# Banded attention and a gated convolution layer: a rewritten schedule, the convolution in array quarters, q and k over 96 partitions

## The chip, the cores and the metric

The kernel runs on one core of a Trainium2 chip. The core has a TensorE (matmuls, written PE in the profile; its weight loads are PEld), a VectorE (DVE), a ScalarE (ACT), a GpSimd (POOL) and a SyncE (SP), which here only issues DMAs. Each engine executes its own instructions in program order and waits on semaphores for the others. A matmul multiplies a stationary operand of up to 128 rows and 128 columns with a moving operand and writes to PSUM, which has 8 banks of 512 float32 per partition. The metric is the device time of one execution in microseconds, lower is better, as the median of several runs.

## The reference

Attention over 8 batches, 8 heads, 576 positions, head size 64, then a gated layer over the 512 channels that the heads make together. Heads 0 to 3 look at the last 32 positions; heads 4 to 7 look at every fourth position of the last 128, which is again 32 positions.

```python
rel = pos[:, None] - pos[None, :]
mask_plain = (rel >= 0) & (rel < 32)
mask_dil = (rel >= 0) & (rel < 128) & (rel % 4 == 0)
scores = np.where(mask, q @ k.T / 8, -1e9)          # mask by head
x = (softmax(scores) @ v)                           # heads side by side: [8, 576, 512]
for kk in range(5):                                 # causal, one weight per channel and tap
    gate_pre += conv_w[kk] * xp[:, kk:kk + 576, :]
gate = 1 / (1 + np.exp(-gate_pre))
out = (gate * (x @ w_val)) @ w_out
```

Inputs and output are float32. The kernel computes in bfloat16 with float32 accumulation.

## The kernel before

The unit of attention is a pair: one batch and two neighbouring heads, so that two times 64 channels fill 128 partitions. There are 32 pairs, four in each batch, two plain and two dilated (`is_dil`). Because a dilated head sees only positions of its own remainder modulo 4, its 576 positions fall into four sequences of 144, in each of which it is a plain band of 32.

`load_qk` and `load_v` bring the next pair but one from SyncE. q and k come as 144 rows of four positions (1,024 bytes each), the first 96 rows on 96 partitions and the other 48 in a second tile, for the dilated pairs with a DMA for each head. Plain v comes in rows of one position (256 bytes). `convert` casts on GpSimd: q and k of the plain pairs, v of the dilated ones. The others are used without a cast: `hi_bf16` views the upper half of each float32 as bfloat16.

`transpose_in` turns q and k so that channels lie on partitions: eight TensorE transposes for each of q and k of a plain pair (four of 96 rows, four of 48), six of 96 rows for a dilated one, then a copy from PSUM (L179 on ScalarE for plain k, L182 on VectorE else). `scores` multiplies k and q, one matmul for each head on its own 64 rows of the array, takes the exponential (L212) and multiplies with the mask (L219); each pair has two halves, `hf`. `attn_v` multiplies with v, which has a column of ones for the sum, and divides (L251, L256). `transpose_x` turns the result back to channels on partitions: six transposes of 96 rows for a plain pair (L275), and for a dilated one four of 96 rows and four of 48 in turns (L269, L271), then a copy to `xT` (L278).

The gated layer works on groups of up to 512 positions. `conv_unit` computes 128 channels of the convolution: for each of five taps a matmul with a diagonal 128 by 128 matrix (L303), then the gate as a tanh (L307). `val_unit` is the product with `w_val` (L315) and the multiplication with the gate (L320). `out_unit` multiplies 128 positions with `w_out` (L329), evicts with ScalarE (L332) and stores from ScalarE's queue (L333).

Order is given by hand: each step of the loop issues the loads of pair i + 2, the scores of pair i, some items of the gated layer (`fill`, by a budget of 3.2 for each step and a cost for each kind), the product with v, the transposes of pair i + 1, again some items, and `transpose_x`. What is left of the gated layer follows after the loop. PSUM has two tiles of two banks for scores and products with v, and four single banks for all else.

Of the kernel before, what the change touches and what calls it, by code (L numbers as in the profile page):

```python
# [11 lines left out]


def _ceil_div(a, b):
    return (a + b - 1) // b


def hi_bf16(ap: bass.AP) -> bass.AP:
    b = ap.bitcast(BF16)
    idx = tuple([slice(None)] * (len(b.shape) - 1) + [slice(1, None, 2)])  # L20
    return b[idx]


@with_exitstack
def kernel(
# [16 lines left out]
    R = 4  # L42
    W = 32
    TT = S // R
    P0, P1 = 96, TT - 96
    scale = 1.0 / float(D) ** 0.5
    NCH = Dm // 128
    NG = H // 2
    NT = S // 96
    SB = S + 4  # L50
    CB = B * SB
    NTOK = B * S
    HALF = 288

    consts = ctx.enter_context(tc.tile_pool(name="consts", bufs=1))
    inbuf = ctx.enter_context(tc.tile_pool(name="inbuf", bufs=4))
    work = ctx.enter_context(tc.tile_pool(name="work", bufs=3))
    moe_sb = ctx.enter_context(tc.tile_pool(name="moe_sb", bufs=6))
    outbuf = ctx.enter_context(tc.tile_pool(name="outbuf", bufs=4))
    ps_s = ctx.enter_context(tc.tile_pool(name="ps_s", bufs=2, space=bass.MemoryType.PSUM))  # L60
    ps_m = ctx.enter_context(tc.tile_pool(name="ps_m", bufs=4, space=bass.MemoryType.PSUM))

    def bank(dt=FP32):
        return ps_m.tile([128, 512 if dt == FP32 else 1024], dt, name="bank")


    NKT_, NVP, NVD, NET = 3, 3, 2, 4
    kTs = [consts.tile([128, 640], BF16, name=f"kT{i}") for i in range(NKT_)]
    ets = [consts.tile([128, 2, 384], BF16, name=f"et{i}") for i in range(NET)]
    vps = [consts.tile([128, NT, 2, D + 1], FP32, name=f"vp{i}") for i in range(NVP)]  # L70
    vd0 = [consts.tile([96, 2, R, D + 1], BF16, name=f"vda{i}") for i in range(NVD)]
    vd1 = [consts.tile([80, 2, R, D + 1], BF16, name=f"vdb{i}") for i in range(NVD)]
    xT = consts.tile([128, NCH, CB], BF16, name="xT")
    y_all = consts.tile([128, NCH, NTOK], BF16, name="y_all")

    ident_b = consts.tile([128, 128], BF16, name="ident_b")
    ident_f = consts.tile([8, 8], FP32, name="ident_f")
    mask_d = consts.tile([128, HALF], BF16, name="mask_d")
    mask_p = consts.tile([128, 2, HALF], BF16, name="mask_p")


    order = [(b, g) for b in range(B) for g in ((2, 3, 0, 1) if b == 0 else (0, 2, 1, 3))]
    nat = {}
    cnt = {"p": 0, "d": 0}
# [4 lines left out]
    def load_qk(i):  # L89
        b, g = order[i]  # L90
        t = {}
        for name, src in (("q", q), ("k", k)):
            rows = src[b, 2 * g:2 * g + 2].rearrange("h (p r) d -> p h (r d)", r=R)
            a = inbuf.tile([P0, 2, R * D], FP32, name=f"{name}a")
            nc.sync.dma_start(out=a, in_=rows[0:P0])
            if is_dil(i):
                z = inbuf.tile([2 * P1, R * D], FP32, name=f"{name}zd")
                for hh in range(2):
                    nc.sync.dma_start(out=z[hh * P1:(hh + 1) * P1], in_=rows[P0:TT, hh, :])
            else:  # L100
                z = inbuf.tile([P1, 2, R * D], FP32, name=f"{name}zp")
                nc.sync.dma_start(out=z, in_=rows[P0:TT])
            t[name] = (a, z)
        nat[i] = t

    def load_v(i):
        b, g = order[i]
        t = nat[i]
        if g >= NG // 2:
            rows = v[b, 2 * g:2 * g + 2].rearrange("h (p r) d -> p h (r d)", r=R)  # L110
            a = inbuf.tile([96, 2, R * D], FP32, name="va")
            nc.sync.dma_start(out=a, in_=rows[0:96])
            z = inbuf.tile([80, 2, R * D], FP32, name="vz")
            nc.sync.dma_start(out=z, in_=rows[64:144])
            j = cnt["d"] % NVD
            cnt["d"] += 1
            t["v"] = (a, z, vd0[j], vd1[j])
        else:
            vt = vps[cnt["p"] % NVP]
            cnt["p"] += 1  # L120
            vv = v[b, 2 * g:2 * g + 2]
            nc.sync.dma_start(out=vt[:, 0, :, 0:D],
                              in_=vv[:, 0:128, :].rearrange("h p d -> p h d"))
            for hh in range(2):
                nc.sync.dma_start(
                    out=vt[:, 1:NT, hh, 0:D],
                    in_=bass.AP(tensor=v.tensor,
                                offset=v.offset + ((b * H + 2 * g + hh) * S + 64) * D,
                                ap=[[D, 128], [96 * D, NT - 1], [1, D]]))
            t["v"] = (vt,)  # L130

    def convert(i):
        if is_dil(i):
            a, z, c0, c1 = nat[i]["v"]
            for src, dst in ((a, c0), (z, c1)):
                nc.gpsimd.tensor_copy(  # L136
                    dst[:, :, :, 0:D], src.rearrange("p h (r d) -> p h r d", r=R))
        else:
            for name in ("q", "k"):
                res = []  # L140
                for src, n, x in zip(nat[i][name], (P0, P1), "az"):
                    c = work.tile([n, R, 2, D], BF16, name=f"{name}c{x}")
                    nc.gpsimd.tensor_copy(
                        c.rearrange("p r h d -> p h r d"),
                        src.rearrange("p h (r d) -> p h r d", r=R))
                    res.append(c)
                nat[i][name] = tuple(res)

    def transpose_in(i, name):
        a, z = nat[i][name]
        ps = bank(BF16)
        if is_dil(i):
            av, zv = hi_bf16(a), hi_bf16(z)
            pv = ps[:, 0:S].rearrange("p (f h t) -> p f h t", f=2, h=2)
            for f in range(2):
                cols = slice(f * 128, f * 128 + 128)
                for hh in range(2):  # L160
                    nc.tensor.transpose(out=pv[:, f, hh, 0:P0], in_=av[:, hh, cols],
                                        identity=ident_b[0:P0, 0:P0])
                nc.tensor.transpose(out=pv[:, f, :, P0:TT], in_=zv[:, cols],  # L163
                                    identity=ident_b[0:2 * P1, 0:2 * P1])
        else:
            for r in range(R):
                nc.tensor.transpose(out=ps[:, r * TT:r * TT + P0],
                                    in_=a[:, r, :, :].rearrange("p h d -> p (h d)"),
                                    identity=ident_b[0:P0, 0:P0])
            for r in range(R):  # L170
                nc.tensor.transpose(out=ps[:, r * TT + P0:(r + 1) * TT],  # L171
                                    in_=z[:, r, :, :].rearrange("p h d -> p (h d)"),
                                    identity=ident_b[0:P1, 0:P1])
        if name == "k":
            dst = kTs[i % NKT_]
        else:
            dst = work.tile([128, S], BF16, name="qT")
        if name == "k" and not is_dil(i):
            nc.scalar.copy(out=dst[:, 0:S].rearrange("p (t r) -> p t r", r=R),  # L179
                           in_=ps[:, 0:S].rearrange("p (r t) -> p t r", r=R))  # L180
        else:
            nc.vector.tensor_copy(dst[:, 0:S], ps[:, 0:S])  # L182
        nat[i][name + "T"] = dst

    state = {}

    def scores(i, hf):
        b, g = order[i]
        dil = g >= NG // 2
        qT, kT = nat[i]["qT"], nat[i]["kT"]  # L190
        ps = ps_s.tile([128, 2, 512], FP32, name="sc")
        qr = qT.rearrange("p (r t) -> p r t", r=R)

        def mm(out_c, ln, lhs, rhs):
            for x in range(2):
                rb = slice(x * D, x * D + D)
                nc.tensor.matmul(out=ps[:, x, out_c:out_c + ln], lhsT=lhs[rb], rhs=rhs[rb],  # L197
                                 start=True, stop=True)
        if dil:
            for hh in range(2):  # L200
                o = (2 * hf + hh) * TT
                mm(hh * 96, 96, kT[:, o:o + 128], qT[:, o:o + 96])
            for hh in range(2):
                o = (2 * hf + hh) * TT
                mm(192 + hh * 48, 48, kT[:, o + 64:o + 192], qT[:, o + 96:o + TT])
        else:
            for c in range(3):
                t = 3 * hf + c
                k0 = 0 if t == 0 else 96 * t - 32
                mm(c * 96, 96, kT[:, k0:k0 + 128], qr[:, :, 24 * t:24 * t + 24])  # L210
# [261 lines left out]
    while queue:  # L472
        run_item()
# [30 lines left out]
```

## Time and profile before

| what | value |
|---|---|
| three runs | 228.67, 231.15, 233.42 us (median 231.15) |
| profiled execution, span from first to last instruction | 223.8 us |
| ScalarE exponentials, L212 | 64 of 660 ns |
| VectorE masks, L219 | 64, median 458 ns |
| VectorE division, L256 | 32 of 686 ns, 32 of 553 ns |
| copies from PSUM: L278, L179 (ScalarE), L182 (VectorE) | 637, 638, 444 ns |
| tanh L307, eviction L332 (ScalarE), product with the gate L320 (VectorE), each 128x512 | 599, 601, 679 ns |
| GpSimd casts of 96x512, L136 and L143 | 622 to 662 ns |
| SyncE issues of loads | 240 |
| ScalarE issues of stores | 36 |

The profile is of one execution; its time as the host measures it is not recorded beside its span. The median of the runs lies 7.35 us above the span. "Busy" is time in which an engine had at least one instruction under way. A TensorE matmul's own duration contains the time that its results take to arrive, so the rate of a stream is read from one start to the next and not from the duration of one. The clock row tells what share of its full clock TensorE was granted.

### The profile page before, as it was taken

Reading aid. Unit: us, or ns where it says so; the run is one execution under the profiler, and the core shown is the slowest. Engines: PE = TensorE matmul, PEld = TensorE weight load, DVE = VectorE, ACT = ScalarE, POOL = GpSimd, SP = SyncE. Lnnn points to the kernel's source line nnn. Section 1 sums busy time; section 2 is a strip of 40 time slices with the busy share of each in tenths; the row PEclk is TensorE's granted clock in tenths of the full one; section 3 lists DMA queues with packets and bytes.
Section 4 is the critical chain, followed back from the end, with each engine's and each line's share of the span. In section 5 each row is a group of like instructions: output and inputs, shape, how many; then the busy total and the mean of one; then the engine's idle time right before and its main releaser. Section 6 shows DMA issues by size and latency. Waiting matters only on the chain.

```text
span 223.8 us, 5850 instructions
## 1 busy us (share of the span) xinstructions
PE 189.1 (85%) x2279; PEld 127.0 (57%) x2292; DVE 128.4 (57%) x311; ACT 108.7 (49%) x190; POOL 65.0 (29%) x123
## 2 busy tenths in 40 slices
PE   2666689878988898898898898889888988999992
PEld 0544545545655576556775686558655666454670
DVE  2566664775667556663666659656776566532320
ACT  2234444356554655475544753465536654643442
POOL 4296506420516150524146024602360200000000
PEclk9999999999999999996999999999999999999999
DMA  5799999747779799869989779778986300221232
GB/s 144 240 220 207 236 216 225 211 120 232 213 212 231 234 254 224 217 222 258 233 192 243 234 217 237 181 244 227 232 213 212 118 3 0 99 91 47 100 141 94
DMA packets 58757, 41.82 MB, mean 187 GB/s; under 512 B 29029, under 2 KB 54117, under 8 KB 58730
## 3 DMA queue, kind: packets, MB, share of 16 engines
q1 hardware_dynamic: 52480, 30.95, 56.1%
q10 hardware_dynamic: 5194, 9.45, 11.8%
q0 software_dynamic: 1056, 1.05, 2.9%
q8 instruction: 18, 0.29, 0.6%
q14 instruction: 9, 0.07, 0.1%
HBM read 33.04 MB, written 9.44 MB: 190 GB/s over the span
## 4 chain that ended last, share of the span: by engine, by line
PE 45%; DMA 15%; ACT 13%; DVE 10%; issue 7%; SPq 6%; ACTq 2%; POOL 0%; DVEq 0%
PE bank L303 16%; ACT et L212 9%; PE bank L315 8%; PE bank L329 5%; DVE et L219 4%; ACT osb L332 4%; DMA qa<-in_q_dram 4%; DVE xn L256 4%; DMA vp<-in_v_dram 3%; PE bank L269 3%; PE sc L246 2%; PE bank L271 2%; DMA ka<-in_k_dram 2%; ACTq L333 2%; DMA kzd<-in_k_dram 2%
## 5 line engine op out<-in xcount | busy, mean ns | idle before, releaser
L303 PE MATMUL bank<-xT,conv_diag 128*128 128x320 bf16 (+7 forms) x319 | 46.3, 295 | 0.3 <-DMA kzd<-in_k_dram 0.3
L256 DVE TENSOR_TENSOR xn<-sc,rec 96x512 bf16<-96x512 f32 (+1 forms) x64 | 39.7, 620 | 2.2
L212 ACT ACTIVATE et<-sc 128x576 bf16<-128x576 f32 x64 | 38.5, 660 | 4.8 <-PE sc L197 4.8
L307 ACT ACTIVATE gate<-bank 128x512 bf16<-128x512 f32 (+3 forms) x40 | 22.0, 556 | 32.8 <-PE bank L303 32.8
L315 PE MATMUL bank<-xT,w_val_b 128*128 128x320 bf16 (+7 forms) x254 | 37.1, 285 | 0.3 <-issue 0.3
L136 POOL CAST vda<-va 96x512 bf16<-96x512 f32 x16 | 10.0, 622 | 92.9 <-DMA va<-in_v_dram 79.3
L332 ACT ACTIVATE osb<-bank 128x512 f32<-128x512 f32 x36 | 21.6, 601 | 29.4 <-PE bank L329 23.4
L320 DVE SCALAR_TENSOR_TENSOR y_all<-gate,bank 128x512 bf16<-128x512 bf16 (+3 forms) x40 | 25.1, 628 | 18.0 <-PE bank L315 9.1
L303 PEld LDWEIGHTS <-conv_diag 128*128 128x128 bf16 x320 | 27.8, 100 | 12.6 <-issue 1.4
L329 PE MATMUL bank<-w_out_b,y_all 128*128 128x512 bf16 x134 | 33.7, 380 | 0.8 <-DVE y_all L320 0.2
L219 DVE TENSOR_TENSOR et<-et,mask_d 128x576 bf16<-128x576 bf16 x32 | 16.7, 524 | 27.9 <-ACT et L212 26.9
L278 ACT COPY xT<-bank 128x576 bf16<-128x576 bf16 x32 | 20.4, 637 | 23.1 <-PE bank L271 17.8
L219 DVE TENSOR_TENSOR et<-et,mask_p 128x576 bf16<-128x576 bf16 x32 | 16.8, 532 | 25.6 <-ACT et L212 24.6
L315 PEld LDWEIGHTS <-w_val_b 128*128 128x128 bf16 x256 | 20.8, 97 | 8.1
L329 PEld LDWEIGHTS <-y_all 128*128 128x128 bf16 x144 | 12.8, 98 | 14.4 <-DVE y_all L320 1.8
L179 ACT COPY kT<-bank 128x576 bf16<-128x576 bf16 x16 | 10.2, 638 | 20.4 <-PE bank L171 16.4
L236 PE MATMUL sc<-vda,et 96*128 96x65 bf16 x128 | 12.2, 203 | 7.6 <-DVE et L219 3.7
L246 PE MATMUL sc<-vp,et 128*128 128x65 bf16 x192 | 12.1, 201 | 7.5 <-DVE et L219 4.2
L269 PE MATMUL bank<-ident_b,xn 96*128 96x96 bf16 x64 | 14.1, 221 | 4.4 <-DVE xn L256 4.4
L251 DVE RECIPROCAL rec<-sc 96x8 f32<-96x8 f32 (+1 forms) x64 | 12.2, 191 | 9.5 <-PE sc L246 7.7
L182 DVE COPY qT<-bank 128x576 bf16<-128x576 bf16 x32 | 14.2, 444 | 3.3 <-PE bank L163 3.0
L236 PEld LDWEIGHTS <-et 96*128 96x128 bf16 x128 | 8.1, 100 | 14.1 <-DVE et L219 13.6
(62 smaller groups left out, 243.5 us busy)
## 6 DMA issues: line engine op xcount, KB each, us to landing
out_dram<-osb ACTq DMA_DIRECT2D x36, 256.0 KB, 2.3
qa<-in_q_dram SPq DMA_DIRECT2D x32, 192.0 KB, 4.1
ka<-in_k_dram SPq DMA_DIRECT2D x32, 192.0 KB, 3.4
vp<-in_v_dram SPq DMA_DIRECT2D x32, 160.0 KB, 3.8
va<-in_v_dram SPq DMA_DIRECT2D x16, 192.0 KB, 3.6
vz<-in_v_dram SPq DMA_DIRECT2D x16, 160.0 KB, 3.8
qzd<-in_q_dram SPq DMA_DIRECT2D x32, 48.0 KB, 3.4
kzd<-in_k_dram SPq DMA_DIRECT2D x32, 48.0 KB, 3.1
```

What stands on the lines that cost most here:

```text
L212: nc.scalar.activation(out=et[:, :, 0:HALF], in_=ps[:, :, 0:HALF], func=AF.Exp, scale=scale)
L219: nc.vector.tensor_tensor(out=ev, in0=ev, in1=for_mask, op=ALU.mult)
L236: nc.tensor.matmul(out=ps[:, x, hh * DA:(hh + 1) * DA], lhsT=et[0:96, x, hh * 96:hh * 96 + 128], rhs=c0[:, hh, r, :], start=True, stop=True)
L256: nc.vector.tensor_tensor(out=xo, in0=av[:, :, :, 0:D], in1=rec[:, :, 0:n, None].to_broadcast([96, 2, n, D]), op=ALU.mult)
L269: nc.tensor.transpose(out=pv[:, r, 0:96], in_=xn[:, 2 * r, :, :].rearrange("p h d -> p (h d)"), identity=ident_b[0:96, 0:96])
L278: nc.scalar.copy(out=xT[:, g, c0:c0 + S].rearrange("p (t r) -> p t r", r=R), in_=pv.rearrange("p r t -> p t r"))
L303: nc.tensor.matmul(out=ps[:, o:o + ln], lhsT=conv_diag[:, c, kk, :], rhs=xT[:, c, s:s + ln], start=(kk == 0), stop=(kk == K - 1))
L307: nc.scalar.activation(out=gate[:, 0:n], in_=ps[:, 0:n], func=AF.Tanh, scale=0.5)
L315: nc.tensor.matmul(out=ps[:, o:o + ln], lhsT=w_val_b[:, mc, c * 128:(c + 1) * 128], rhs=xT[:, mc, col:col + ln], start=(mc == 0), stop=(mc ...
L320: nc.vector.scalar_tensor_tensor(out=y_all[:, c, t0:t0 + n], in0=gate[:, 0:n], scalar=1.0, in1=ps[:, 0:n], op0=ALU.add, op1=ALU.mult)
L329: nc.tensor.matmul(out=ps[0:n, :], lhsT=y_all[:, c, t0:t0 + n], rhs=w_out_b[:, c, :], start=(c == 0), stop=(c == NCH - 1))
L332: nc.scalar.activation(out=osb[0:n, :], in_=ps[0:n, :], func=AF.Copy, scale=0.5)
```

## The change

The kernel is written anew. The costs that stand in its code are figures of its planner and are not used as times here. The list of its parts:

- **Order.** Each piece of work is a `Task` with a cost, dependencies, a priority and a number of PSUM banks. `Plan.run` places the tasks one after the other on a model of the engines and picks the engine where a task may run on two; the program is emitted in that order. It models SyncE's queue too, with at most eight transfers in flight.
- **PSUM.** One tile of eight banks; a task takes one bank or any two and gives them back after its eviction.
- **Loads.** q and k lie on 96 partitions: dilated in rows of 12 positions (3,072 bytes), plain in rows of six (1,536 bytes), one DMA each; six buffers for each of q and k, where there were four. Plain v's first block has 96 rows where it had 128.
- **Attention.** Six transposes of 96 rows for each of q and k, of both kinds. k is reordered when it is copied from PSUM, in the dilated pairs also. One mask multiplication of 1,152 columns for a pair, in place of two of 576; VectorE or GpSimd. The division of a plain pair is one operation over six blocks. `transpose_x` of a dilated pair has eight transposes of 96 rows.
- **Gated layer.** It goes by whole batches in halves of 288 positions. The convolution uses 64 by 64 diagonal matrices: rows 0 to 63 and 64 to 127 of the array, for each the columns of one of the two halves, so that four matmuls address four quarters. In the second half of positions the two halves of the 128 channels are exchanged, and `w_val` and `w_out` are kept in a second, exchanged copy for it. The output takes four tiles of 128 positions for each batch, and after four batches two more made of the 32 positions that each half leaves.
- **Stores.** From SyncE's queue, between the loads; 36 as before, and two DMAs that make the exchanged `w_out`. SyncE issues 144 loads, 36 stores and these two. ScalarE or VectorE evicts the output and q, k and x.

```diff
+class Plan:
+    def run(self):
...
+                    e = min(t.cost, key=lambda e: max(ready, free[e]) + t.cost[e])
+                    est = max(ready, free[e])
+                    if e == "SP":
+                        live = sorted(x for x in flight if x > est)
+                        if len(live) >= self.FLIGHT:
+                            est = live[-self.FLIGHT]
...
+    PS = psum.tile([128, 8, 512], FP32, name="ps")
...
+    NQ, NV, NET, NX, NO = 6, 4, 3, 3, 6
...
+    order = [(b, g) for b in range(B) for g in ((2, 0, 3, 1) if b == 0 else (0, 2, 1, 3))]
...
+            if dil:
+                s = two.rearrange("h (p r) d -> (h p) (r d)", r=12)
+                d = dst
+            else:
+                s = two.rearrange("h (p r) d -> p h (r d)", r=6)
+                d = dst.rearrange("p (h c) -> p h c", h=2)
+            P["l" + nm] = ld("ld" + nm, i + (0.0 if nm == "q" else 0.1), 295.0, 300.0,
+                             lambda t, d=d, s=s: nc.sync.dma_start(out=d, in_=s), [dep])
...
+    def transpose_in(t, i, src):
+        ps = bank(t, BF16)
+        if is_dil(i):
+            for f in range(6):
+                nc.tensor.transpose(out=ps[:, f * 96:f * 96 + 96],
+                                    in_=hi_bf16(src)[:, f * 128:f * 128 + 128],
+                                    identity=ident[0:96, 0:96])
+        else:
+            for j in range(6):
+                nc.tensor.transpose(out=ps[:, j * 96:j * 96 + 96],
+                                    in_=src[:, j, :, :].rearrange("p h d -> p (h d)"),
+                                    identity=ident[0:96, 0:96])
...
+    def exps(t, ps, et, hf):
+        nc.scalar.activation(out=et[:, hf * 576:hf * 576 + 576].rearrange("p (b c) -> p b c", b=2),
+                             in_=ps[:, :, 0:HALF], func=AF.Exp, scale=scale)
+    def masks(t, i, et):
+        eng = nc.vector if t.engine == "DVE" else nc.gpsimd
+        eng.tensor_tensor(out=et[:, 0:ET], in0=et[:, 0:ET], in1=(mask_d if is_dil(i) else mask_p)[:, 0:ET],
+                          op=ALU.mult)
...
+    def transpose_x(t, i, xn, xm):
+        ps = bank(t, BF16)
+        if is_dil(i):
+            for part in (1, 0):
+                sv = (xn, xm)[part].rearrange("p n h d -> p (n h d)")
+                for rho in range(2):
+                    for hf in range(2):
+                        o = (rho * 2 + hf) * 128
...
+                        nc.tensor.transpose(out=dst, in_=sv[:, o:o + 128], identity=ident[0:96, 0:96])
...
+        mk = P["mk"] = add("mk", i, {"DVE": 1.05, "POOL": 2.4}, lambda t: masks(t, i, et),
+                           exs + [K_sd if dil else K_sp])
...
+    def conv(t, b, c):
+        ps = banks(t, 2)
+        for kk in range(K):
+            for half in range(2):
+                for x in range(2):
+                    ob = (x ^ half) * D
+                    s = b * SB + half * HALF + kk
+                    nc.tensor.matmul(out=ps[ob:ob + D, half, 0:HALF],
+                                     lhsT=conv_d[x * D:x * D + D, c, kk, :],
+                                     rhs=xT[x * D:x * D + D, c, s:s + HALF],
+                                     start=(kk == 0), stop=(kk == K - 1))
+    def val(t, b, c):
+        ps = banks(t, 2)
+        for half in range(2):
+            s = b * SB + 4 + half * HALF
+            for mc in range(NCH):
+                nc.tensor.matmul(out=ps[:, half, 0:HALF], lhsT=w_val[half][:, mc, c * 128:(c + 1) * 128],
+                                 rhs=xT[:, mc, s:s + HALF], start=(mc == 0), stop=(mc == NCH - 1))
...
+    def out_tile(prio, half, cols, deps, store):
...
+        ot = add("ot", prio, {"PE": 0.87}, lambda t: outp(t, half, cols), list(deps) + K_wo[half], banks=1, mode="full")
+        oe = add("oe", prio, {"ACT": 0.60, "DVE": 0.69}, lambda t: evict_o(t, bank(ot), osb),
+                 [ot] + (out_st[n - NO] if n >= NO else []), frees=[ot])
+        sts = [add("st", prio, {"SP": 0.45}, lambda t, e=e: e(osb), [oe], lag=(nb, 340.0)) for e, nb in store]
...
+    def gated(b):
+        base = 4 * b + 3
...
+            cv = add("conv", base + 1.0 + 0.5 * c, {"PE": 0.62}, lambda t, c=c: conv(t, b, c), [ev[c], K_cd], banks=2, mode="half")
...
+            vl = add("val", base + 1.2 + 0.5 * c, {"PE": 0.98}, lambda t, c=c: val(t, b, c), list(ev.values()) + K_wv, banks=2, mode="full")
...
+    for b in range(B):
+        for i in range(4 * b, 4 * b + 4):
+            attend(i)
+        gated(b)
+    for t in plan.run():
+        t.emit(t)
```

## The prediction, made before the changed kernel ran

> **What bounds the kernel now.** I read the slices of the span first, then busy times by stage, the chain of waits, and single stretches of TensorE.
>
> ```profile
> PE   2666689878988898898898898889888988999992
> PEclk9999999999999999996999999999999999999999
> DMA  5799999747779799869989779778986300221232
> ```
>
> Three phases: a start in which the DMA row is full and PE is not, a long middle with PE at 8 to 9, and an end with PE full and DMAs nearly idle. The stages, cut where each batch's convolution starts (columns: stretch, length, then busy us of each engine, clock, DMA share, GB/s):
>
> ```profile
> 0.00:32.00 32.00, 18.65 (x229) 13.28 (x231) 18.61 (x62) 10.69 (x18) 16.20 (x43) 1.00 0.98 209
> 55.80:79.30 23.50, 21.00 (x290) 13.25 (x284) 14.85 (x34) 12.72 (x23) 8.30 (x13) 1.00 0.79 224
> 102.20:127.30 25.10, 22.90 (x296) 16.42 (x293) 14.98 (x34) 13.12 (x23) 8.83 (x15) 0.94 0.95 243
> 195.40:223.80 28.40, 23.82 (x146) 13.85 (x146) 7.35 (x15) 11.19 (x22) 0.00 (x0) 1.00 0.25 93
> ```
>
> The span is 32.0 + 7 periods of 23.34 + 28.4. In a period PE is busy 21.0 of 23.5 us, VectorE 14.9, ScalarE 12.7: PE bounds the middle, with DMAs at 0.79 behind it. The first batch waits for loads; the end is gated-layer work left over. The chain in a period and at its end (start, us, what):
>
> ```profile
> 55.94 2.30 PE bank L303 x20
> ...
> 59.15 0.87 PE bank L315 x8
> 60.02 1.10 PE bank L303 x10
> ...
> 63.81 0.17 PE bank L167 x4
> 63.98 0.20 PE bank L171 x4
> 64.18 0.28 PE bank L167 x4
> 64.46 0.20 PE bank L171 x4
> ```
>
> The convolution costs 1.10 us for 512 positions and 128 channels, val 0.87. PE alone, start, duration, line:
>
> ```profile
> 60.96 0.42 PE L275 MATMUL bank<-ident_b,xn 96*128 96x96 bf16 x6
> 61.31 0.44 PE L197 MATMUL sc<-qT,kT 64*128 64x96 bf16 x16
> 61.69 0.29 PE L315 MATMUL bank<-xT,w_val_b 128*128 128x64 bf16 x4
> ...
> 197.14 0.21 PE L269 MATMUL bank<-ident_b,xn 96*128 96x96 bf16 x1
> 197.28 0.19 PE L271 MATMUL bank<-ident_b,xn 48*128 48x48 bf16 x1
> 197.41 0.22 PE L269 MATMUL bank<-ident_b,xn 96*128 96x96 bf16 x1
> ```
>
> Six transposes of 96 rows last 0.42 us; one lasts 0.21, so they start 0.042 us apart. The sixth starts at 61.17 and the first score at 61.31, 0.14 later: going over to 64 rows costs about 0.10. L269 and L271 pay this at every step, since 48 rows take the 64-row form: they start 0.13 to 0.14 apart.
>
> **The change part by part**, against the span, in us of each period (one batch: two plain pairs, two dilated, 576 positions of the gated layer).
>
> *Convolution.* Now 4 x 1.10 x 576/512 = 4.95. In quarters, if all four run side by side, half the columns: 2.48. The row that it is nearest to is L197: 16 matmuls on two row halves, 0.44 in all, less a last one of about 0.18, is 0.26, or 0.033 for each pair of 96 and 48 columns in turn, with both weight loads: two halves do run together. Four quarters no row shows. The bounds: two at a time, 4.95, no gain; four, a gain of 2.47. For weight loads the nearest row is L315 with 64 columns: four loads and matmuls with starts 0.03 apart, (0.29 - 0.19)/3; four loads of a tap would take 0.12 beside 288 columns that take 0.215 x 288/512 = 0.12 (val's 0.87/4 for 512), just hidden. I take four. Eight changes of form at 0.10 are added at most (0.8), none if each convolution stands beside scores; I take 0.5. Gain 1.97; lower bound a loss of 0.8.
>
> The page "TensorEngine Tiling (Array Packing)", section Restrictions and Gotchas, says that column tiling excludes fast weight loads, and "TensorE: Matmul & The Clock Gate", section LDWEIGHTS, gives columns / 1.2 ns without them: by estimate 53 ns for 64 columns, 213 for the four of a tap if one follows the other, which would make the convolution 4.3 and the gain 0.2. The first page also says that different row tiles cannot access one PSUM bank at the same time; here the two row tiles of a half do write one bank, on different partitions. No run here shows either in quarters.
>
> *Transposes.* Of dilated x: eight that take 1.09 (197.14 to the next item at 198.23) become eight of 96 rows, 0.34: 0.75 twice, 1.5. Of plain q and k: 0.17 + 0.20 + 0.28 + 0.20 = 0.85 become 12 x 0.042 = 0.50: 0.35 twice, 0.7. Dilated ones stay at 12.
>
> *Val, output, scores, products with v* keep their columns: nothing on PE. Output has 36 tiles as before.
>
> PE: 21.0 - 1.97 - 1.5 - 0.7 = 16.8 a period. With the 2.5 that it is now idle, 19.3; with convolution at its bounds 18.3 to 22.1.
>
> *VectorE.* Masks 8 x 0.53 become four of 1,152 columns, about 2 x 0.458 each: -0.5; dilated k goes from L182 (0.444) to a reordering copy like L179's: -0.9 if ScalarE takes it, +0.4 (0.638 each) if not. *ScalarE* gains those 2 x 0.638, loses 4.5 issues of 0.35. Both stay under 15.5 of a period and hide behind PE as long as that is over 16. If a mask goes to GpSimd, no row shows it; by its casts (0.62 for 512 columns) it takes 1.4, behind the next pair's scores, and is late only if v's product has nothing ahead of it. *GpSimd* casts: 96 rows of 768 columns, 0.93, four in place of eight of 0.64: less, never a bound.
>
> *DMAs.* Bytes stay near 5.2 MB a period, packets get longer for q and k.
>
> ```profile
> q1 hardware_dynamic: 52480, 30.95, 56.1%
> q10 hardware_dynamic: 5194, 9.45, 11.8%
> ```
>
> Loads: 30.95 MB in 0.561 x 223.8 = 125.6 us of full engines, 246 GB/s; stores with 2,048-byte rows: 9.45 MB in 26.4, 358 GB/s. All queues take 71% of the span, 158. The 18.9 MB of q and k cost 77 at the first rate and 53 at the second; so DMAs take 134 to 158, 16.8 to 19.8 a period, and at the share 0.95 of the third stage 17.7 to 20.8. I take the middle, 19.2, as the new packets lie between the two rows.
>
> PE and DMAs then stand equal, and neither can be full all the time: period 20.2, one over 19.2. Ends: 18.8 (both at their lower bounds, and a little) and 22.6 (DMAs without gain plus 1.8, as now).
>
> *SyncE* issues 182 DMAs at 0.44 instead of 240, 80 of the span. But a store waits there for its eviction, and all later loads wait behind it; their readers are transposes up to six pairs later. I cost it at nothing because loads run ahead by six buffers instead of four; without that cover, see below. The two DMAs that exchange `w_out` wait there for its load, 7.4 from issue to landing, once; if loads have not run ahead by then, the first period is that much longer.
>
> *Constants.* The exchanged `w_val` is 2,048 columns copied, by L278's 0.637 for 576 some 2.3, once; the diagonal matrices are one operation of 1,280 columns, by the mask's 0.458 for 576 some 1.0, in place of 20 of 0.29 (L401). Both fall into the start, where VectorE is busy 18.6 of 32: nothing.
>
> *Start.* Four pairs are 3.83 MB, 18.3 at 209 GB/s, 0.8 for the first issue, 3 to land, 5 for the last pair's own chain of copies, exponentials and division: 27, where it was 32 (30 issues of SyncE by 13.4 become 13 for the first three pairs). Ends 24 and 30.
>
> *End.* The last batch's layer: val 3.9, output 6 x 0.88, half of the convolution and switches 3, first product 0.7, eviction, issue and landing 0.6 + 0.44 + 2.3: 16.2, and 0.8 of older work: 17, where it was 28.4 (two batches). Ends 14 and 19.
>
> Sum: 27 + 7 x 20.2 + 17 = 185.4; with the 7.35 between span and median, 192.8.
>
> **Rivals.**
>
> *Quarters run two at a time, or longer rows bring nothing.* PE: 16.8 + 2.47 + 2.5 = 21.8 a period; DMAs without gain: up to 22.6. Then 27 + 7 x 21.8 + 18 + 7.35 = 205, to 211. For it: no row has four quarters, and each queue row mixes packet sizes. Against: the row halves of L197 do overlap.
>
> *Both limits lie lower than I take them:* all of q and k at the stores' rate and PE without the switches: 18.3 a period, 24 + 128.1 + 15 + 7.35 = 174.5. For it: L197 pays its switch once for 16 matmuls. Against: DMAs at 0.95 were reached in one period only.
>
> *SyncE's order holds up the loads, slower than before.* 4.5 stores a period stand in front of loads; when PE lags the plan, evictions come late, loads behind them start late, and with DMAs near full they cannot catch up, which makes PE lag more. For it: evictions L332 waited 23.4 us in all, at most 2.6, for L329, and DMAs have 1 us of slack in 20.2 where they now have nearly 5. Against: six buffers. It decides from 235.8 (2% above 231.15), a period of (235.8 - 7.35 - 27 - 17)/7 = 26.3: 6.1 lost in each, 1.36 for each store.
>
> **How the numbers follow.** The runs before spread 1% to each side of the median, so 2% (4.6 us) is what can be told. The forecast, 178 to 200 (periods 18.8 to 21.2 with the sum's other terms): 0.60. First rival, 200 to 213: 0.20. Faster than 178: 0.05. Between 213 and 226.5: 0.02. Within 2%: 0.03. Slower: 0.10. So faster is 0.60 + 0.20 + 0.05 + 0.02 = 0.87, and the range 178 to 213 leaves out 0.20.
>
> **What would show it.** Convolution: the ten matmuls of one half of positions and both row halves start in groups of four, groups 0.12 apart (0.24 if two at a time). Dilated x: starts 0.042 apart. q and k loads: a higher GB/s at full DMA share than 256. Period between the batches' last copies to `xT`: 20.2. A long wait of SyncE for an eviction of the output, with PE idle for a load after it, would show the slower rival. I would be wrong if VectorE or ScalarE stood at 9 in the slices.

## The result, and the profile after

The changed kernel takes 278.28 us (median of four runs, 276.30 to 279.38) where the kernel before takes 229.91 in the same comparison: a ratio of 1.220, 95% interval 1.209 to 1.231. It is slower, against the forecast. The profiled execution has a span of 274.3 us.

The slices of the span, after (busy tenths of PE, granted clock, DMA share):

```profile
PE   3667567858678658587585778787887577677860
PEclk9999999977997955959759579999779799979995
DMA  7999991195974599305899017788999240003041
```

PE stands at 5 to 8 where it stood at 8 to 9, the DMA row has holes down to 0, and the clock row, nearly flat before, falls to 5. No engine is full: busy PE 190.6 us (69% of the span), VectorE 120.7 (44%), ScalarE 118.4 (43%). PE's busy time did not fall (189.1 before) although its work did, as will be seen. Two lists of waits, after, who waits for whom, with the total, the number and the longest, first of the engines, then of SyncE's queue:

```profile
DVE et L408 <- ACT et L403: 26.5, 18, 5.9
...
ACT et L403 <- PE ps L547: 11.7, 10, 1.9
...
DVE rec L436 <- ACT gate L599: 6.9, 3, 5.0
...
DVE rec L436 <- ACT osb L570: 5.8, 3, 3.8
...
PE ps L547 <- ACT et L403: 5.8, 8, 1.9
```

```profile
SPq L617 <- ACT osb L570: 125.6, 28, 17.2
```

Two things stand out, and they make two theories. The first list has pairs that exchange nothing: the reciprocal of the softmax sums (L436) needs the product with v, not the gate's tanh (L599) nor an eviction of the output (L570), which both only read PSUM; the exponential (L403) needs scores, not the convolution (L547). The second line is what my slower rival spoke of: SyncE waited 125.6 us for evictions of the output, with all later loads behind them. A moment of the first kind, in order of time (start, duration, what, and in brackets the idle time before it and what ended it):

```profile
100.49 1.42 PE L547 MATMUL ps<-xT,conv_d 64*64 64x288 bf16 x20
...
102.01 0.65 ACT L403 ACTIVATE et<-ps 128x576 bf16<-128x576 f32 x1 [0.98 <-PE ps L547]
...
102.72 0.82 PE L417 MATMUL ps<-vp,et 128*128 128x65 bf16 x12 [0.81 <-ACT et L403]
...
103.57 0.65 ACT L599 ACTIVATE gate<-ps 128x576 bf16<-128x576 f32 x1 [0.91 <-PE ps L417]
104.25 0.23 DVE L436 RECIPROCAL rec<-ps 96x12 f32<-96x12 f32 x1 [5.03 <-ACT gate L599]
104.27 1.12 PE L557 MATMUL ps<-xT,w_val 128*128 128x288 bf16 x4 [0.74 <-ACT gate L599]
```

In the program this exponential reads banks 1 and 7, and the product with v writes banks 3 and 4; the gate reads 0 and 6, the reciprocal 3 and 4, and val writes 2. PE waits 0.81 and 0.74 us, VectorE 5.03, at the end of a row of such waits, and none of the pairs shares a bank. But the ranges from first to last bank overlap each time. I compared every semaphore wait between the computing engines in the compiled program with the banks and addresses of the two instructions: of 753, 266 join instructions that have nothing in common, and all 266 join ranges of banks that overlap. No such count had been made for the prediction.

Theory F is that these waits cost the time. Theory S is that the stores in front of the loads do. Theory P is that the plan's times are too short for the hand-overs between engines, so that reuse of banks really stalls.

### The profile page after: what moved, and what is told of

It is laid out like the page before. It is cut to its first block, busy times and chain, and to the rows that moved or that the text cites. A ratio compares the mean times of both kernels' runs of the same rounds, so it can differ in the third digit from the quotient of the medians.

```text
span 274.3 us, 6193 instructions
## 1 busy us (share of the span) xinstructions
PE 190.6 (69%) x2548; PEld 131.0 (48%) x2548; DVE 120.7 (44%) x213; ACT 118.4 (43%) x196; POOL 58.3 (21%) x104
## 4 chain that ended last, share of the span: by engine, by line
PE 55%; DVE 20%; ACT 15%; issue 4%; DMA 2%; SPq 1%; POOL 0%; ACTq 0%; DVEq 0%
PE ps L557 13%; PE ps L565 11%; PE ps L547 10%; ACT et L403 8%; DVE xn L437 6%; DVE y L603 6%; PE ps L400 5%; PE ps L351 3%; ACT gate L599 3%; PE ps L356 3%; PE ps L417 3%; DVE xm L437 3%; DVE rec L436 2%; PE ps L454 2%; DMA q<-in_q_dram 2%
## 5 line engine op out<-in xcount | busy, mean ns | idle before, releaser
L403 ACT ACTIVATE et<-ps 128x576 bf16<-128x576 f32 x64 | 39.9, 650 | 38.8 <-PE ps L400 17.1
L557 PE MATMUL ps<-xT,w_val 128*128 128x288 bf16 x256 | 42.5, 317 | 7.3 <-DVE xn L437 2.5
L565 PE MATMUL ps<-w_out,y 128*128 128x512 bf16 x128 | 38.5, 438 | 3.5 <-DVE xm L437 1.2
L547 PE MATMUL ps<-xT,conv_d 64*64 64x288 bf16 x640 | 34.1, 344 | 8.1 <-ACT et L403 5.8
L603 DVE SCALAR_TENSOR_TENSOR y<-gate,ps 128x576 bf16<-128x576 bf16 x32 | 23.8, 752 | 30.1 <-PE ps L557 19.9
L557 PEld LDWEIGHTS <-w_val 128*128 128x128 bf16 x256 | 26.4, 108 | 18.4 <-issue 10.0
L570 ACT ACTIVATE osb<-ps 128x512 f32<-128x512 f32 x34 | 20.3, 597 | 23.5 <-PE ps L565 22.9
L599 ACT ACTIVATE gate<-ps 128x576 bf16<-128x576 f32 x32 | 20.6, 652 | 22.1 <-PE ps L547 10.4
L436 DVE RECIPROCAL rec<-ps 96x8 f32<-96x8 f32 (+1 forms) x48 | 10.0, 209 | 45.2 <-ACT gate L599 6.9
L547 PEld LDWEIGHTS <-conv_d 64*64 64x64 bf16 x640 | 21.5, 125 | 13.6 <-issue 9.3
L437 DVE TENSOR_TENSOR xn<-ps,rec 96x512 bf16<-96x512 f32 (+1 forms) x32 | 26.2, 820 | 1.1
L565 PEld LDWEIGHTS <-y 128*128 128x128 bf16 x128 | 12.4, 108 | 18.8 <-issue 10.8
L362 ACT COPY xT<-ps 128x576 bf16<-128x576 bf16 x20 | 12.8, 639 | 19.3 <-PE ps L458 15.6
```

What stands on the lines that cost most here:

```text
L362: nc.scalar.copy(out=out_, in_=in_)
L403: nc.scalar.activation(out=et[:, hf * 576:hf * 576 + 576].rearrange("p (b c) -> p b c", b=2), in_=ps[:, :, 0:HALF], func=AF.Exp, scale=scale)
L436: nc.vector.reciprocal(out=rec[:, :, 0:n], in_=av[:, :, :, D])
L437: nc.vector.tensor_tensor(out=xo, in0=av[:, :, :, 0:D], in1=rec[:, :, 0:n, None].to_broadcast([96, 2, n, D]), op=ALU.mult)
L547: nc.tensor.matmul(out=ps[ob:ob + D, half, 0:HALF], lhsT=conv_d[x * D:x * D + D, c, kk, :], rhs=xT[x * D:x * D + D, c, s:s + HALF], start= ...
L557: nc.tensor.matmul(out=ps[:, half, 0:HALF], lhsT=w_val[half][:, mc, c * 128:(c + 1) * 128], rhs=xT[:, mc, s:s + HALF], start=(mc == 0), st ...
```

## The experiments

### Neighbouring banks, and the same plan with other names

```diff
                         elif t.banks == 2:
-                            a, b = sorted(idx[:2])
-                            bank = (a, b - a)
+                            bank = min(((a, 1) for a in (0, 2, 4, 6)),
+                                       key=lambda p: (max(bank_free[p[0]], bank_free[p[0] + 1]), p))
```

> Edit: a task that needs two PSUM banks takes only the pairs (0,1), (2,3), (4,5), (6,7), where the changed kernel takes any two free ones. Theory F (false waits): an access to two banks that are not neighbours is held to touch all banks between them, so that engines wait for each other over banks that they do not share; the program of the changed kernel has 266 such waits between the computing engines among 753, this one has none. F expects the median to fall from 278 to between 195 and 225, the span's PE busy share from 69% to over 80% and the granted clock from 0.87 to over 0.97. Theory S (stores in front of loads on SyncE): nothing changes there, 270 to 285. Theory P (the planner's times are too short for the hand-overs between engines, so real reuse of banks stalls): fewer choices of banks, so the same or slower, 275 to 295.

The second kernel keeps this plan and renames the banks: pair 2p, 2p + 1 becomes p, p + 4.

```diff
     def banks(t, n, dt=FP32):
-        b, s = t.bank
+        b, s = t.bank[0] // 2, 4
...
-        return (PSB if dt == BF16 else PS)[:, t.bank[0], :]
+        return (PSB if dt == BF16 else PS)[:, t.bank[0] // 2 + 4 * (t.bank[0] % 2), :]
```

> The same order of instructions on every engine as in the kernel with neighbouring pairs, and the same sharing of banks between tasks; only the numbers of the banks differ: pairs (0,4), (1,5), (2,6), (3,7). The program then has 426 waits over banks that are not shared. Theory F expects the worst time of all, 280 to 330. Theories S and P expect the time of the kernel with neighbouring pairs, within 2%, since nothing but names has changed.

Measured: 196.39 us with neighbours (ratio to before 0.863, interval 0.856 to 0.870) and 346.57 with the distant names (1.525, 1.506 to 1.543). Every engine has the same instructions in the same order in both, and each bank is shared by the same tasks. So S and P, which expect no difference, cannot account for 150 us, and the waits over banks that are not shared do. Nor is it that reading two distant banks is slow in itself: the mean exponential lasts 653 ns with neighbours and 650 with the distant names. The waits number 0, 266 and 426 in the three programs, with 196, 278 and 347 us: 0.31 and 0.35 us for each. The moment above makes that size plausible: each of its two waits of PE lasts 0.7 to 0.8 us, about one operation of ScalarE, and some waits are hidden. One thing F expected did not come: with neighbours the granted clock rose to 0.94 to 0.96, not to over 0.97.

The distant kernel's slices:

```profile
PE   2577566777768475756776875766648855675780
PEclk9999997656567859995555599886675788569886
DMA  8999910287803695079700455489900120001032
```

It is the picture of the changed kernel, only more so: idle PE, a falling clock, holes in the DMA row. Since only names differ between this kernel and the one with neighbours, all three are consequences of the waits.

### Is it the stores in front of the loads?

In the changed kernel and in the one with neighbouring pairs the same edit puts the 36 stores back on ScalarE's queue:

```diff
-        sts = [add("st", prio, {"SP": 0.45}, lambda t, e=e: e(osb), [oe], lag=(nb, 340.0)) for e, nb in store]
+        sts = [add("st", prio, {"ACT": 0.36}, lambda t, e=e: e(osb), [oe], lag=(nb, 340.0)) for e, nb in store]
...
-                         [(lambda osb, t0=t0: nc.sync.dma_start(out=out[b, t0:t0 + 128, :], in_=osb), 262.0)]))
+                         [(lambda osb, t0=t0: nc.scalar.dma_start(out=out[b, t0:t0 + 128, :], in_=osb), 262.0)]))
```

> The changed kernel with one edit: its 36 stores go out from ScalarE's queue as before, so that no load stands behind an eviction of the output. Any two free banks are still taken, and the program has 273 waits over banks that are not shared (266 in the changed kernel). Theory S, by the 125.6 us that SyncE waited for those evictions: below 255. Theory F: 265 to 300, since the waits stay; more than the changed kernel's 278 if ScalarE, blocked by a store, holds up its exponentials as it did with neighbouring pairs (208.0 against 196.4).

> Neighbouring pairs, and the 36 stores issued from ScalarE's queue as in the kernel before. Theory F with stores at no cost: within 2% of the kernel with neighbouring pairs, as loads run up to six pairs ahead. Theory S: 4% or more faster than that kernel, with no stretch of the DMA row under 3 in the middle, where the changed kernel's SyncE waited 125.6 us for evictions of the output.

Measured: the changed kernel 281.5 (ratio 1.232, 1.218 to 1.245), the one with neighbouring banks 207.99 (0.914, 0.907 to 0.922) where it had 196.39. S falls: without its cause the changed kernel is no faster, and its program still has 273 waits over banks that are not shared. F's expectation for the second run was a miss: stores from ScalarE cost 11.6 us there. Its timeline of ScalarE shows at least one way:

```profile
92.61 0.60 ACT L570 ACTIVATE osb<-ps 128x512 f32<-128x512 f32 x1
96.78 0.34 ACTq L617 DMA_DIRECT2D out_dram<-osb  x1
97.17 0.64 ACT L362 COPY xT<-ps 128x576 bf16<-128x576 bf16 x1 [3.96 <-DMA out_dram<-osb]
```

The store waits for an earlier DMA to land before it can be issued, and ScalarE, with copies queued behind it, stands for 3.96 us. On SyncE only loads stand behind such a wait. So SyncE is the better place for the stores here, although its queue shows the larger waits. How much of the 11.6 us is this, and how much the other plan that the edit makes, was not taken apart.

### The convolution in quarters

```diff
-            for half in range(2):
-                for x in range(2):
-                    ob = (x ^ half) * D
-                    s = b * SB + half * HALF + kk
-                    nc.tensor.matmul(out=ps[ob:ob + D, half, 0:HALF],
-                                     lhsT=conv_d[x * D:x * D + D, c, kk, :],
-                                     rhs=xT[x * D:x * D + D, c, s:s + HALF],
+            for half in range(2):
+                s = b * SB + half * HALF + kk
+                nc.tensor.matmul(out=ps[:, half, 0:HALF], lhsT=conv_d[:, c, kk, :],
+                                 rhs=xT[:, c, s:s + HALF],
                                  start=(kk == 0), stop=(kk == K - 1))
```

> Neighbouring pairs, and the convolution on the full array: 320 matmuls of 128 rows and columns and 288 positions in place of 640 of 64 by 64; no exchange of halves. The changed kernel's 20 matmuls of one unit took 0.74 to 0.81 us in its chain, the full array would take 10 x 0.124 = 1.24 by val's rate. If PE bounds the kernel with neighbouring pairs, this one is 32 x 0.45 = 14 us slower than that, 7% at 200; if hand-overs or DMAs bound it, less than 4 us slower.

Measured: 196.57 (0.866, 0.859 to 0.873) against 196.39. The quarters bring nothing there. To see whether that is because they don't work or because something else binds, the same pair was run with most of v's loads left out, on pairs of neighbouring banks at any place (called the repaired kernel below):

```diff
+                            bank = min(((a, 1) for a in range(7)),
+                                       key=lambda p: (max(bank_free[p[0]], bank_free[p[0] + 1]), p))
...
+        if j >= (3 if dil else NV):
+            P["lv"] = [None, None, None]
+        elif dil:
```

> Pairs of neighbouring banks at any place, (0,1), (1,2) and so on, where the kernel with neighbouring pairs has four fixed ones. No wait over a bank that is not shared, as there. Theory F expects the same within 3% (190 to 202); if scarcity of banks holds that kernel up, 5 us or more faster. It is also the base of the two kernels without later loads of v.

> As the one before, but v is loaded only for the first pairs that fill each of its buffers (three dilated, four plain); later pairs use what lies there, so their product with v is of older data. This takes some 9 MB of 33 MB of reads away and no work of any engine except the issues. If DMAs bound the kernel with neighbouring pairs (its DMA row stands at 9 for 165 us at 210 to 250 GB/s), the time falls by 20 us or more, to 165 to 178. If PE or the order binds, it stays within 6 us of the base.

> As the one before, with the convolution on the full array. With DMAs out of the way the quarters must show: this one slower by 14 us (32 units by 1.24 less 0.80) if PE then binds. Within 4 us of it if quarters bring nothing on any path, as in the pair of runs in which the two kernels stood at 196.4 and 196.6.

Measured: the base 195.41 (195.04 in a later repeat), without later v 186.69, without it and with the full array 195.33. Their ratios to the kernel before, in one comparison, are 0.854, 0.812 and 0.857, each to about 0.01. So the loads hold the base up by 8.7 us by the medians and some 10 by the ratios, less than the 20 I expected. With them lighter the quarters are worth 8.6 by the medians and some 10 by the ratios, where I expected 14. Each of the three has its own plan. PE alone, in order of time; first a unit in quarters in the repeat of the base, then one on the full array without later v, each with what follows it:

```profile
105.74 0.81 PE L547 MATMUL ps<-xT,conv_d 64*64 64x288 bf16 x20
106.48 0.43 PE L458 MATMUL ps<-ident,xn 96*128 96x96 bf16 x6
```

```profile
105.45 1.40 PE L547 MATMUL ps<-xT,conv_d 128*128 128x288 bf16 x10
106.69 0.41 PE L429 MATMUL ps<-vda,et 96*128 96x65 bf16 x8
```

From its start to the next item a unit takes 0.74 in quarters, change of form included, and 1.24 on the full array. Twice as many matmuls in 0.6 of the time run four side by side; two at a time would need 1.24 too. In the records of that unit they start in fours, each four within 10 ns and the next 0.12 to 0.15 us later, as the prediction asked. The 32 units save 16 us by this, the change of form in front of them not counted; without later v PE's busy time is 155.8 in quarters and 168.5 on the full array, 12.7 apart, and most of that reaches the end. How much of the rest goes into changes of form was not measured.

### The planner's rates

The last stretch of the kernels with neighbouring banks is gated-layer work with the DMAs nearly idle, so the plan might be wrong about loads.

```diff
-            P["l" + nm] = ld("ld" + nm, i + (0.0 if nm == "q" else 0.1), 295.0, 300.0,
+            P["l" + nm] = ld("ld" + nm, i + (0.0 if nm == "q" else 0.1), 295.0, 225.0,
...
-        sts = [add("st", prio, {"SP": 0.45}, lambda t, e=e: e(osb), [oe], lag=(nb, 340.0)) for e, nb in store]
+        sts = [add("st", prio, {"SP": 0.45}, lambda t, e=e: e(osb), [oe], lag=(nb, 700.0)) for e, nb in store]
```

> Neighbouring pairs, and the planner told that loads move at 225 GB/s (it has 220 to 300) and stores at 700, since reads alone moved 226 to 228 in the second to fourth slice of that kernel. If its last 34 us (DMAs nearly idle, PE full) come from gated-layer work that the fixed order put behind late loads, the plan puts more of it in between and the time falls by 5 to 15 us. If the order is no worse for the wrong rates, it stays within 2%.

Measured: 201.72 (199.74 to 205.63), against 196.39 (195.67 to 201.59): no gain. The lowest runs of the two lie 4 us, 2%, apart, so that a loss is not shown either. More truthful rates for the DMAs alone do not give a better order, and a few us between two plans of the same tasks say little about the edit that made them.

### Row length

```diff
+            n = 3 if dil else 2
+            w = d.shape[-1] // n
+            for m in range(n):
+                cut = (slice(None),) * (len(d.shape) - 1) + (slice(m * w, m * w + w),)
```

> Neighbouring pairs at any place, and each load of q and k cut into shorter rows: three DMAs of 1,024 bytes a row for a dilated pair, two of 768 for a plain one. The bytes are the same, the packets as short as those of the kernel before, 96 issues more on SyncE (some 43 us of its time, beside 195). If longer rows are worth what the prediction took (12 us of engine time of all DMAs), the time rises by 8 us or more over 195.4 with the DMA row full for longer. If a limit on reads together sets the pace whatever the row, it stays within 3%.

> Neighbouring pairs at any place once more, as the base of the runs beside it: 192 to 198 by every theory.

Measured: 208.15 with short rows, 195.04 with the long ones. The time rose as the first reading expected, but not for its reason: the DMA row is less full than before, not longer full. The load queue's line, first with short rows, then with long ones in the repeated base (packets, MB, share of 16 engines over the span):

```profile
q1 hardware_dynamic: 59824, 40.65, 72.7%
```

```profile
q1 hardware_dynamic: 46000, 40.64, 86.6%
```

With spans of 205.2 and 192.8 that is 0.727 x 205.2 = 149 us of engine time for short rows and 0.866 x 192.8 = 167 for long ones, for the same bytes. So the longer packets did not spare engine time here; why they took more of it is not shown. What 96 more issues and their order cost is mixed into the 13 us, and the worth of the longer rows is not settled.

## Why the prediction was wrong, step by step

**The step that failed** is "With the 2.5 that it is now idle, 19.3": I took PE's idle time of a period from the old schedule and kept it. PSUM had no term in my sum, though the change puts all of it into one tile with two-bank slices, and none of my rivals was a wait between tasks that share nothing. Cut at the batches' last copies to `xT`, the 274.3 us of the changed kernel are 34.0 + 7 x 31.41 + 20.4, where the sum had 27 + 7 x 20.2 + 17. Of a period of 31.4 PE is idle for 8.5 and busy for 22.9, where the sum had 2.5 and 16.8. The repeat of the repaired kernel is 28.9 + 7 x 20.53 + 20.2, with PE idle for 1.9 of a period and busy for 18.6: without these waits the 2.5 would have been enough. The runs put their price at 82 us (278.3 against 196.4 with neighbouring pairs); what the other plan, which the edit also makes, has in these 82 was not taken apart, but with nothing changed except names such waits cost 150.

**Where the 82 us went.** Compare the changed kernel with the repeat of the repaired one, by their busy PE, with the same 2,548 matmuls in the program: 190.6 against 158.7 us, so 32 us more busy; and idle 274.3 - 190.6 = 83.7 against 192.8 - 158.7 = 34.1, 50 us more. The repaired kernel's slices:

```profile
PE   1387968987999989995999999479998999999900
PEclk9999999999999999999699999969999999999995
DMA  6999999998999999999999987699999960050431
```

The idle part is the waits. Most of the busy part is the clock: its mean is 0.869 against 0.969. While PE has work, the clock is at half for 64.8 us in the changed kernel, with PE busy for 54.2 of them, and for 6.8 in the repaired one, busy for 6.4. The unit of the convolution at the head of the moment above shows 1.42 us at half clock, the one at 105.74 in the repaired kernel 0.81 at full clock. By an estimate that takes half of the busy time at half clock as added, the clock makes 24 of the 32 us; the other 8 were not taken apart. In two stretches of the changed kernel, one after the other (columns as in the stages above, clock, DMA share and GB/s last):

```profile
55.50:58.90 3.40, 1.26 (x20) 0.95 (x20) 1.63 (x3) 1.73 (x4) 0.00 (x0) 0.99 0.88 216
58.90:65.70 6.80, 5.97 (x45) 2.98 (x46) 2.00 (x5) 1.90 (x4) 2.74 (x4) 0.50 0.77 195
```

PE is busy in 1.26 of 3.4 us, and then runs 6.8 us at half clock. So waits are in part paid for twice: as idle time, and as slow work after it. That waits bring the clock down is shown by the names alone: 0.94 to 0.96 with neighbours, 0.76 to 0.79 with distant pairs.

**The slower rival** named the right side and the wrong mechanism. SyncE did wait for evictions far longer than I priced (125.6 us), yet taking the stores away from it changed nothing (281.5). The waits of SyncE were an effect of late evictions: with neighbouring pairs and the same queue they are 24.6 us.

**The convolution** was right in mechanism: four quarters run side by side, 0.74 a unit with its change of form, where the sum had 0.62 and 0.12 for its share of changes. The Trainium skill spoke against it: column tiling excludes fast weight loads ("TensorEngine Tiling (Array Packing)", Restrictions and Gotchas), and with the load time of "TensorE: Matmul & The Clock Gate", LDWEIGHTS, one unit would by estimate take 1.07 us if the four loads of a tap followed one another. That does not decide here: the 20 weight loads of a unit fit into the 0.74. Nor does the sentence of the first page's section that different row tiles cannot access one bank at the same time: two row tiles that write different partitions of one bank start within 10 ns of each other. That the gain shows in no time with all loads in place, 196.4 against 196.6, I had not foreseen for that term, though I had DMAs level with PE.

**The transposes** were right. In the repeat of the repaired kernel (PE alone, start, duration):

```profile
111.75 0.34 PE L454 MATMUL ps<-ident,xm 96*128 96x96 bf16 x4
111.93 0.33 PE L454 MATMUL ps<-ident,xn 96*128 96x96 bf16 x4
112.10 0.42 PE L351 MATMUL ps<-ident,q 96*128 96x96 bf16 x6
```

Eight dilated ones take 112.10 - 111.75 = 0.35 (0.34 in the sum, 1.09 before).

**The DMA term** was mis-sized. I had 134 to 158 us of full engines; the changed kernel used 0.639 x 274.3 = 175. The rate of 358 GB/s that I took from the stores' queue as an end for long rows belongs to the stores. With neighbouring banks and the stores on ScalarE's queue, loads and stores have a line each:

```profile
q1 hardware_dynamic: 40864, 31.20, 67.2%
q10 hardware_dynamic: 5146, 9.45, 13.3%
```

The loads, with their longer rows, move 31.20 MB in 0.672 x 205.8 = 138 us, 226 GB/s where the kernel before had 246; the stores 9.45 MB in 27.4, 345 GB/s. From 20 to 120 us, with a DMA share of 1.00 to 1.17, the repaired kernel moves 248 to 264 GB/s in all, the kernel before 243 at 0.95. PE and the DMAs then both stand near full, as the sum had them:

```profile
60.00:80.00 20.00, 18.82 (x335) 13.99 (x338) 15.32 (x28) 13.88 (x24) 6.14 (x9) 1.00 1.09 264
100.00:120.00 20.00, 19.64 (x347) 13.75 (x348) 14.47 (x24) 15.56 (x27) 5.74 (x9) 1.00 1.00 251
```

**What the rewrite would have been worth.** With neighbouring banks it takes 195.0 to 196.4 us, 0.855 (0.848 to 0.861) of the kernel before in the repeat, and beats both kernels. That this lies near my 192.8 is in part luck. The repeat's span is 192.8 where my sum of the span was 185.4: start and end were 1.9 and 3.2 too low, the periods together 2.3. The 7.35 that I added from span to median hides this. It was mis-sized: wherever a run's own span is on record, its time lies 1.7 to 2.0 above it.

Two bounds of the prediction were slips. With the convolution at its best PE's period comes to 18.8, not 18.3, and the second rival to 178.0, not 174.5. And a period of 18.8 with the sum's other terms gives 183, not 178. Neither bears on the result.

Not tried: the old hand-written order with the new pieces, which would tell what the list scheduler itself brings, and free pairs of banks with evictions cut into single banks.

## What to carry to other kernels

When tiles are merged into one and handed out by hand, ask what the dependence tracking sees of a slice with a step: here a two-bank slice counted as all banks between, and neighbouring banks were worth 82 us. Count the waits of the compiled program that join instructions with nothing in common before trusting a schedule, and test it by renaming: a change of names that alters no order must not alter the time. A long wait on a queue that runs ahead is often an effect; move the queue before blaming it.

## What the runs showed of the hardware

The TensorE clock fell to half after a stretch of 3.4 us in which PE was still busy for 1.26, so an entirely idle stretch was not needed. The same 2,548 matmuls kept PE busy for 158.7, 190.6 and 225.7 us at mean clocks of 0.969, 0.869 and 0.764 in the repaired, the changed and the renamed kernel. The same 40.6 MB took 149 us of the DMA engines' time with short rows of q and k and 167 with long ones.
